# Attention, mixer and MLP on one core: weight chunks, mixer transposes and the first output projection put into later slots

## The chip, the core and the metric

The kernel runs on one core of a Trainium2 chip. Its engines work side by side, each on its own queue of instructions: TensorE (PE, matrix products into PSUM), VectorE (DVE), ScalarE (ACT), GpSimd (POOL) and SyncE (SP). POOL and SP here mostly issue DMAs; the DMAs of both run on the same 16 DMA engines. The metric is the device time of one execution in microseconds, the median of several runs. The kernel before: 818.71 us (three runs, 818.16 to 819.41).

## The reference

A normalised input feeds an attention branch and a mixer-and-MLP branch; the output is the input plus the product of the two.

```python
x = A_x                                     # 2048 tokens x 576
xn = layernorm(x)
# attention: 32 query heads, 16 key/value heads, Dh = 128, the last W = 512 keys of the cache
q = (xn @ wq) by heads
p = softmax(q @ k^T * Dh**-0.5)
s = (p @ v, heads side by side) @ wo        # 4096 -> 576
# mixer and MLP
h  = gelu(layernorm(xn) @ w1)
hs = (four quarters of h shifted by +1, -1, +2, -2 tokens) @ w2
x1 = xn + hs
g  = silu(x1 + gelu(layernorm(x1) @ w3) @ w4)
out = x + s * g
```

## The kernel before

**Blocks and slots.** The 2048 tokens are cut into four blocks (NB = 4) of 512 (QB), each of four tiles (TB) of 128. The attention part is a loop over slots u = 0 to 128, one for each head of each block: Hq = 32 heads, so block b has slots 32 b to 32 b + 31. Slot u has the scores and exponentials of head u (`stage_s`, L545 and L549), the query projection of head u + 1 (`stage_q`, L526, with its rest of 64 rows for four heads at a time in `rest_q`, L511), and the product with the values of head u - 1 (`stage_v`, L564, normalised by DVE at L568 and L569 into an `o` tile).

**What is hung into the slots.** `at(u, fn)` puts work into slot u, `pe(u, atoms)` puts PE work there. The order on SP, POOL and PE is the program's (L723); DVE and ACT are ordered by the framework's scheduler in this part. The lists that the change touches:
- `load_wq(j)` (L335) loads the query weights of four heads, 512 KB and two pieces of 32 KB, into one of two buffers, by POOL in slot 4 (j - 1) - 1. It can go as soon as the last reading of that buffer is over, one slot earlier.
- `load_wo(i)` (L410) loads an eighth of the output projection's weights, 576 KB, by POOL, in slots 9, 13, 17, ... 37 (L673). It goes through `late` (L242): a tiny POOL copy first waits for the first exponential of that slot, and POOL's later DMAs wait behind it.
- `load_k` and `load_v` bring keys and values. The last two groups of four key heads are loaded in slots 4 and 12 into a `stage` buffer, and transposed by DMA from SP in slots 9 to 12 and 17 to 20 (`tr_k`, L380).
- `stage_t(u)` (L574) transposes the `o` tile of a head by DMA from SP into one of 36 `oT` buffers, for the output projection. How many of them are issued in a slot is counted out in L709 to L722: one, two from slot 38 on, and never more than 36 before the first projection is over. There are 18 `o` buffers.
- `wo_groups` (L264): the output projection of a block, four groups of 32 matmuls 512 wide and one of 128 that are 64 wide, each in one slot. The first block's are in slots WO0 = Hq + 11 = 43 to 47, the next ones' in 65 to 69 and 97 to 101. Within a slot the matmuls are dealt out in three parts; the first group already needs all 32 heads and all eight weight chunks.
- `ln2_apply` (L206, two DVE instructions for each tile) normalises a block for the mixer into `xm_b`, and `tr2` (L257) transposes it by DMA from SP. For blocks 0 and 1, `tr2_at` is 34 and 42: the normalisation is written two slots earlier, and the result stays in a `stage` buffer until the mixer. Blocks 2 and 3 have buffers of their own, filled after the loop.
- `load_x` in slots 14, 44 and 68 (`x_at`) loads the next block's input, by POOL through `late`.

**The mixer** comes after the slots (L889 to L953), in an order written by hand on all engines. A loop over k works through sixteen pairs of PSUM banks: `b1_pair` is a product with w1 and its GELU, `b2_pair` a product with w2. Step k issues the first half of pair k, then what `aside` holds for this k, then the second half of pair k - 1 and its evictions. `b1_rest(b)` in `aside` makes the last 64 columns of block b: small products on PE, two DVE instructions (L845, L846), a GELU on ACT (L847) and a transpose by DMA from SP (L848). The banks come round every three steps, so pair 5 starts when the GELUs of pair 2 have read theirs. In step 3, `b1_rest(3)` and the shift copies of block 0 (L855) stand ahead of the second half of pair 2.

After the mixer the MLP runs in matmuls of 64 rows (L1022, L1059), and the last block in 128 (L1237).

Of the kernel before, what the change touches and what calls it, by code (L numbers as in the profile page):

```python
# [8 lines left out]
P = 128  # L9
ACT = mybir.ActivationFunctionType  # L10
ALU = mybir.AluOpType
AX = mybir.AxisListType
BF16 = mybir.dt.bfloat16
# [18 lines left out]
def kernel(  # L32
# [14 lines left out]
    nc = tc.nc  # L47
# [6 lines left out]
    Hq = A_wq.shape[1] // Dh  # L54
# [7 lines left out]
    QB = 512  # L62
    NB = S // QB
    TB = QB // P
# [3 lines left out]
    NDC = NF + 1  # L68
    DP = NDC * P
    DCH = [(i * P, min(P, D - i * P)) for i in range(NDC)]  # L70
    M0 = 512
    R0 = D - M0
# [4 lines left out]
    OFF = 16  # L77
# [150 lines left out]
    oT_pool = octx.enter_context(tc.tile_pool(name="oT_pool", bufs=OT, side="right"))  # L228
    fence_pool = ctx.enter_context(tc.tile_pool(name="fence", bufs=2))
    tctx = ctx.enter_context(ExitStack())  # L230
    stage_pool = tctx.enter_context(tc.tile_pool(name="stage_pool", bufs=2))
    so_pool = tctx.enter_context(tc.tile_pool(name="so_pool", bufs=1))
    so_t, oT_t, xnnT = {}, {}, {}
    w1_all = xT_b[0][:].rearrange("p k q -> p (k q)")
# [16 lines left out]
                                in_=w1_tail.rearrange("p (j two s) -> p j two s", two=2, s=c4)[:, :, half, 0:P])  # L251
    flag_m = [None]

    def stage():
        return stage_pool.tile([P, DP * TB], BF16, name="stage")

    def tr2(b, tt, home=None):  # L257
        if tt == 0:
            xnnT[b] = (home or stage())[:].rearrange("p (k t) -> p k t", k=NDC)
        nc.sync.dma_start(out=xnnT[b][:, :, tt * P:(tt + 1) * P], in_=xm_b[b % 2][:, tt, :], transpose=True)  # L260

    FLAG_OPS = (ALU.max, ALU.min)
# [36 lines left out]
    with ExitStack() as actx:  # L299
# [50 lines left out]
        kst_t = {}  # L350

        def load_k(i, eng=None, step=4):
            kst_t[i] = stage()
            dst = kst_t[i][:, 0:4 * W].rearrange("p (g a) -> p g a", g=4)
            for g in range(0, 4, step):
                (eng or nc.gpsimd).dma_start(
                    out=dst[:, g:g + step, :],
                    in_=A_k_cache[0, 4 * i + g:4 * i + g + step, K0:, :].rearrange("g (p kc) d -> p g (kc d)", p=P))
# [30 lines left out]
        for tt in range(TB):  # L389
            if tt:  # L390
                (nc.sync if tt < TB - 1 else nc.scalar).dma_start(out=x_first[:, tt, :],
                                                                  in_=x2[tt * P:(tt + 1) * P, :])
# [4 lines left out]
        with tc.manual_schedule(engines={SP}):  # L397
            load_k(0, nc.sync, 2)
            for m0 in (0, 2 * Dh):
                cols = slice(m0, m0 + 2 * Dh)  # L400
                nc.sync.dma_start(out=wq_b[0][:, 0:NF, cols],
                                  in_=A_wq[0:NF * P, cols].rearrange("(kc p) m -> p kc m", p=P))
# [220 lines left out]
            return PLAIN - 1 <= u < U - 1 and u % 4 == 3  # L623

        ln2_at = (7, Hq + 3, 2 * Hq - 4, 2 * Hq + 20)
        tr2_at = (Hq + 2, Hq + 10, 3 * Hq - 10, 3 * Hq - 5)
        WO0 = Hq + 11
        tr_k_at = {u: g for u, g in zip([*range(9, 13), *range(17, 21)], range(KDMA, Hkv))}
        x_at = (14, Hq + 12, 2 * Hq + 4)
        ln1_at = (19, Hq + 21, 2 * Hq + 16)  # L630

        for b in range(1, NB):
# [37 lines left out]
                pe_late.append((2 * g - 3, g))  # L670
        for j in range(2, NB * 8):
            at(4 * (j - 1) - 1, lambda j=j: load_wq(j))
        for i, u in enumerate((9, 13, 17, 21, 25, 29, 33, 37)):  # L673
            at(u, lambda i=i, u=u: late(pT_t[u][0][0:1, 0:1], lambda: load_wo(i)))
        for b in range(NB):
            at((b + 1) * Hq + 1, lambda b=b: row_range(b))
# [33 lines left out]
        for u in range(1, U + 1):  # L710
            n = 1
            if u in tr_k_at:
                turn[u] = [lambda g=tr_k_at[u]: tr_k(g)]
                n = 0
            elif u > Hq + 5:
                n = 2
            if u < WO0 + TB + 1:
                n = min(n, OT - done)
            for _ in range(min(n, u - done)):
                turn.setdefault(u, []).append(lambda v=done: stage_t(v))  # L720
                done += 1
# [28 lines left out]
    with ExitStack() as bctx:  # L750
# [23 lines left out]
        hq = mres.tile([P, HW], BF16, name="hq")  # L774
        hs = mres.tile([P, S], BF16, name="hs")
        h4 = [mres.tile([P, TB, P], BF16, name=f"h4_{i}") for i in range(NB)]
# [61 lines left out]
        def b1_rest(b):  # L838
            def ops(half, tt, k):
                w = w1_m[half, k, :].rearrange("p (g s) -> p g s", g=4)[:, :, P:c4] if k < NF else w1_q[half, :, :]  # L840
                return xnnT[b][half, k, tt * P:(tt + 1) * P], w

            pr = small_products(ops)
            gs = gs_pool.tile([P, TB, R0], FP32, name="gs")
            nc.vector.tensor_copy(out=gs[:], in_=pr[0])  # L845
            nc.vector.tensor_tensor(out=gs[:], in0=gs[:], in1=pr[1], op=ALU.add)  # L846
            nc.scalar.activation(out=h4[b][:, :, 0:R0], in_=gs[:], func=ACT.Gelu_apprx_tanh)  # L847
            nc.sync.dma_start(out=hq[:, OFF + b * QB:OFF + (b + 1) * QB].rearrange("p (t q) -> p t q", t=TB),  # L848
                              in_=h4[b][:].rearrange("p t c -> p (t c)"), transpose=True)

        def shifts(b):
            for g in (1, 0, 3, 2):
# [36 lines left out]
        with tc.manual_schedule(engines={SP, POOL, PE, DVE, ACTE}):  # L889
            for b in range(2, NB):  # L890
                home = mres.tile([P, DP * TB], BF16, name=f"xnnT{b}")
                for tt in range(TB):
                    tr2(b, tt, home)
            e = small.tile([P, 1], FP32, name="nr_e")
            nc.scalar.activation(out=e[:], in_=so_t[NB - 1][:, 1, 0:1], func=ACT.Gelu_apprx_tanh)
            for half in range(2):
                nc.gpsimd.dma_start(out=w1_q[HALVES[half], :, :],
                                    in_=w1_tail.rearrange("p (g s) -> p g s", g=4)[:, :, P:c4])
            for half in range(2):
                for g in range(4):  # L900
                    p0 = half * DR + g * rsz
                    nc.gpsimd.dma_start(out=w2_q[p0:p0 + rsz, :], in_=w2_by_g[g, P:c4, :])
            for t in (hb[:, :, OFF - PAD:OFF], hb[:, :, OFF + S:OFF + S + PAD], hq[:, OFF - PAD:OFF],
                      hq[:, OFF + S:OFF + S + PAD], *[t[:, :, R0:] for t in h4]):
                nc.gpsimd.memset(t, 0.0)
            nc.gpsimd.dma_start(out=mx_dram[:, :], in_=flag_m[0][:])
            nc.gpsimd.dma_start(out=m1[:], in_=mx_dram[:, :].rearrange("(o p) c -> o c p", o=1))
            ops = [(b1_pair, 0), (b1_pair, 1), (b2_pair, 0), (b1_pair, 2), (b2_pair, 1), (b1_pair, 3), (b2_pair, 2),
                   (b2_pair, 3)]
            ops = [(f, b, p) for f, b in ops for p in range(2)]  # L910
            aside = {0: [lambda: b1_rest(0)], 1: [lambda: b1_rest(1)], 2: [lambda: b1_rest(2)],
                     3: [lambda: b1_rest(3), lambda: shifts(0)], 6: [lambda: shifts(1)], 8: [lambda: shifts(2)],
                     10: [lambda: shifts(3)]}
            pend = None
            ln3_0 = ln3_steps(0)
            ln3_at = {7: 2, 8: 1, 11: 3, 12: 3}
            for k in range(len(ops) + 1):
                nxt = None
                if k < len(ops):
                    f, b, p = ops[k]  # L920
                    nxt = f(b, p, bank_pair((("pm0", "pm2"), ("pm1", "pm3"))[k % 3 - 1]) if k % 3 else h3_banks())
                    nxt[0]()
                for fn in aside.get(k, []):
                    fn()
                if pend:
                    pend[1]()
                    f, b, p = ops[k - 1]
                    if f is b2_pair and p == 1:
                        b2_rest(b)
                for _ in range(ln3_at.get(k, 0)):  # L930
                    ln3_0.pop(0)()
                pend = nxt
            while ln3_0:
                ln3_0.pop(0)()
            ln3_transpose(0)
            mm = small.tile([1, 2], FP32, name="mm", bufs=1)
            for k in range(2):
                nc.vector.tensor_reduce(out=mm[:, k:k + 1], in_=m1[:, k, :], axis=AX.X, op=FLAG_OPS[k])
            over = small.tile([1, 1], FP32, name="over", bufs=1)
            nc.vector.tensor_scalar(out=over[:], in0=mm[:, 0:1], scalar1=ROW_LIMIT, scalar2=None, op0=ALU.is_gt)  # L940
            nc.vector.scalar_tensor_tensor(out=flag_i[:], in0=mm[:, 1:2], scalar=1.0 / ROW_LIMIT, in1=over[:],
                                           op0=ALU.is_lt, op1=ALU.add)

            def wo_bank(shape, name):
                if name == "pswr":
                    return ps_h2.tile([P, QB], FP32, name="pr0")[:, 0:TB * R0].rearrange("p (t r) -> p t r", t=TB)
                return ps_h2.tile(shape, FP32, name="pr1" if wo_i else "pm0")

            wo_b = wo_groups(NB - 1, wo_bank, nc.scalar)
            for wo_i, i in enumerate((2, TB, 3)):  # L950
                for atom in wo_b[i]:
                    atom()
            nc.gpsimd.tensor_copy(out=gate[:, :], in_=hs[P // 2:P // 2 + 1, S - 1:S])  # L953
# [194 lines left out]
        with tc.manual_schedule(engines={PE, DVE, ACTE}):  # L1148
# [7 lines left out]
            for d in range(0, ND, 2):  # L1156
                b = d // NP
# [3 lines left out]
                end = d % NP == NP - 2  # L1161
# [52 lines left out]
            b = NB - 1  # L1214
# [59 lines left out]
    with tc.If(flag > 0):  # L1274
        nc.gpsimd.dma_start(out=g_dram[(NT - 1) * P:NT * P, :], in_=g_last)
        with ExitStack() as gctx:
# [20 lines left out]
            with tc.For_i(0, NT, 1) as t:  # L1297
# [10 lines left out]
                with tc.For_i(0, Hq, 1) as h:  # L1308
# [7 lines left out]
                                        in_=A_wq[0:NF * P, cols].rearrange("(kc p) m -> p kc m", p=P))  # L1316
# [72 lines left out]
```

## Time and profile before

| | |
|---|---|
| Median of three runs | 818.71 us (818.16 to 819.41) |
| Profiled execution, whole | 822.13 us |
| its span, first to last instruction | 820.6 us |
| Mean granted PE clock | 0.996 |
| PE busy | 806.4 us, 98% |
| DVE, ACT, POOL busy | 445.1, 445.7, 125.2 us |
| DMA queue of SP and ACT (q1), share of 16 engines | 27.4% |
| DMA queue of POOL (q0) | 18.6% |

How the views read: a view of stretches of time has one row for each stretch: its limits and length in us, then the busy time of PE, PE's weight loads (PEld), DVE, ACT and POOL with their number of instructions, the clock granted to PE as a share of full speed, the busy share of the DMA engines, and GB/s. A row of the timeline has the start in us, the duration in us, engine, line, operation, output and inputs, and how many like instructions are merged; in brackets stand the idle time before it and what ended it. A row of DMA issues has the output and input, the engine that issued it, the number, KB for each, and the median time from issue to landing in us. A row of waits has the sum, the number and the longest. A row by line has the shortest, median and longest duration in ns and the first and last start.

### The profile page before, as it was taken

What the parts mean: (1) busy time and instruction counts of PE and PEld (TensorE: products, weight loads), DVE (VectorE), ACT (ScalarE), POOL (GpSimd) and SP (SyncE); (2) the same over time, 40 slices, a digit from 0 to 9 for tenths busy, and PEclk for the clock granted to TensorE, in tenths of its full rate; (3) what the DMA queues carried; (4) which work ended last, traced back from release to release, by engine and by line L of the source; (5) the groups of instructions that cost most, each with busy time, mean ns of one, the idle gap of its engine ahead of it and who ended that gap; (6) DMA issues with size and microseconds to landing.
All of it is one profiled execution on the core that took longest, in us unless ns stands there. A gap on an engine that the chain in (4) does not pass through costs nothing. (4 is left out here: it accounts for less than half of the span.)

```text
span 820.6 us, 19925 instructions
## 1 busy us (share of the span) xinstructions
PE 806.4 (98%) x8174; PEld 466.8 (57%) x8255; DVE 445.1 (54%) x1383; ACT 445.7 (54%) x798; POOL 125.2 (15%) x211
## 2 busy tenths in 40 slices
PE   8998999999999999999999999999999999999997
PEld 6664665566654656645666645655555555555555
DVE  6877686128831579722566528444246636655413
ACT  7887886248833788833788632033233423334620
POOL 3253221101101111100211211172000000000000
PEclk9999999999999999999999999999999999999999
DMA  8899996029821447520553472399000410320101
GB/s 212 143 204 195 171 190 137 29 66 143 156 67 42 91 105 135 110 49 14 107 130 101 79 99 63 66 324 282 3 2 16 77 59 16 48 88 16 45 15 38
DMA packets 135534, 80.73 MB, mean 98 GB/s; under 512 B 112112, under 2 KB 125712, under 8 KB 135440
## 3 DMA queue, kind: packets, MB, share of 16 engines
q1 hardware_dynamic: 121360, 39.32, 27.4%
q0 software_dynamic: 12832, 38.85, 18.6%
q8 instruction: 65, 1.06, 0.6%
q10 hardware_dynamic: 1248, 1.25, 0.5%
q14 instruction: 29, 0.24, 0.1%
HBM read 46.89 MB, written 6.93 MB: 66 GB/s over the span
## 5 line engine op out<-in xcount | busy, mean ns | idle before, releaser
L549 ACT ACTIVATE pT<-sc 128x512 bf16<-128x512 f32 x512 | 287.1, 599 | 96.4 <-PE sc L545 81.6
L545 PE MATMUL sc<-qT,kT 128*128 128x512 bf16 x504 | 167.6, 379 | 0.2
L564 PEld LDWEIGHTS <-pT 128*128 128x128 bf16 x2048 | 134.6, 98 | 53.2 <-issue 11.4
L564 PE MATMUL po<-v_sb,pT 128*128 128x129 bf16 x2048 | 158.3, 220 | 0.5
L526 PE MATMUL psq<-xT_b,wq_b 128*128 128x512 bf16 x455 | 123.2, 381 | 5.3 <-DMA wq_b<-in_A_wq_dram 2.5
L1022 PE MATMUL ph<-xT_b,w_s 64*128 64x512 bf16 x976 | 127.2, 376 | 0.0
L1059 PE MATMUL pm<-w_s,h 64*128 64x512 bf16 x864 | 122.0, 377 | 0.0
L1040 ACT ACTIVATE h<-ph 128x512 bf16<-128x512 f32 x67 | 39.4, 597 | 132.7 <-PE ph L1022 130.5
L569 DVE TENSOR_TENSOR o<-po,ri_b 128x256 bf16<-128x256 f32 x256 | 107.8, 421 | 6.3
L1059 PEld LDWEIGHTS <-h 64*128 64x128 bf16 x1728 | 70.2, 94 | 55.9
L269 PE MATMUL pswo<-wo_sb,oT 128*128 128x512 bf16 x434 | 101.2, 379 | 0.6
L269 PEld LDWEIGHTS <-oT 128*128 128x128 bf16 x1024 | 64.7, 98 | 54.2
L1059 PE MATMUL pr<-w_s,h 64*128 64x64 bf16 x864 | 89.6, 189 | 0.0
L536 DVE CAST qT<-psq 128x512 bf16<-128x512 f32 x64 | 44.0, 688 | 78.1 <-PE psq L511 45.4
L526 PEld LDWEIGHTS <-wq_b 128*128 128x128 bf16 x506 | 49.5, 98 | 61.2 <-DMA wq_b<-in_A_wq_dram 3.0
L1022 PEld LDWEIGHTS <-w_s 64*128 64x128 bf16 x1152 | 55.4, 94 | 49.0 <-issue 0.6
L534 DVE TENSOR_TENSOR qT<-psq,rq 128x512 bf16<-128x512 f32 x62 | 42.8, 690 | 65.1 <-ACT pT L549 57.9
L1038 DVE COPY hx<-ph 128x512 f32<-128x512 f32 x55 | 38.0, 692 | 60.7 <-PE ph L1022 60.7
L339 POOL DMA_DIRECT2D wq_b<-in_A_wq_dram x30 | 23.1, 770 | 272.1 <-PE sc L545 260.3
L568 DVE RECIPROCAL ri_b<-po 128x2 f32<-128x2 f32 x256 | 42.2, 165 | 37.8 <-PE po L564 32.9
L545 PEld LDWEIGHTS <-kT 128*128 128x128 bf16 x512 | 46.0, 98 | 21.1 <-DVE qT L534 0.4
L516 ACT ACTIVATE rq<-sc 128x512 f32<-128x512 f32 x62 | 33.6, 594 | 11.9 <-PE sc L511 11.9
(171 smaller groups left out, 702.1 us busy)
## 6 DMA issues: line engine op xcount, KB each, us to landing
wq_b<-in_A_wq_dram POOLq DMA_DIRECT2D x30, 512.0 KB, 5.2
wo_sb<-in_A_wo_dram POOLq DMA_DIRECT2D x8, 576.0 KB, 5.9
w_s<-in_B_w_dram POOLq DMA_DIRECT2D x9, 512.0 KB, 6.1
w_s<-in_B_w_dram POOLq DMA_DIRECT2D x10, 288.0 KB, 5.1
w_s<-in_B_w_dram POOLq DMA_DIRECT2D x4, 576.0 KB, 5.8
s_b<-s_dram SPq DMA_DIRECT2D x4, 576.0 KB, 5.4
x_b<-in_A_x_dram SPq DMA_DIRECT2D x4, 576.0 KB, 6.7
out_dram<-o SPq DMA_DIRECT2D x15, 144.0 KB, 1.8
```

What stands on the lines that cost most here:

```text
L269: nc.tensor.matmul(ps, lhsT=oT_t[qb * Hq + h][:, tt, :], rhs=wo_sb[:, h, lo:hi], start=(i == 0), stop=(i == Hq - 1))
L526: nc.tensor.matmul(psq[:, :], lhsT=w[:, kc, hh * Dh:(hh + 1) * Dh], rhs=xT_b[qb % 2][:, kc, :], start=(kc == 0 and not (two and hh == 1)), ...
L534: behind["qT"] = nc.vector.tensor_tensor(out=qT[:, :], in0=psq[:, :], in1=rq_t.pop(u)[:, :], op=ALU.add)
L536: nc.vector.tensor_copy(out=qT[:, :], in_=psq[:, :])
L545: nc.tensor.matmul(sc[:, :], lhsT=kT[:, g, kc * P:(kc + 1) * P], rhs=qT_t[u][:, :], start=True, stop=True)
L549: behind["exp"] = nc.scalar.activation(out=pT[:, :], in_=sc[:, :], func=ACT.Exp, scale=SCALE)
L564: nc.tensor.matmul(po[:, j, :], lhsT=pTs[kc][:, tt * P:(tt + 1) * P], rhs=v_sb[:, g, kc, 0:Dh + 1], start=(kc == 0), stop=(kc == KCH - 1))
L568: nc.vector.reciprocal(out=ri, in_=po[:, :, Dh])
L569: nc.vector.tensor_tensor(out=o[:, t0:t0 + 2, :], in0=po[:, :, 0:Dh], in1=ri.unsqueeze(2).to_broadcast([P, 2, Dh]), op=ALU.mult)
L1022: nc.tensor.matmul(ps[i][:, :], lhsT=lhsT, rhs=xT[half, kc, :], start=first, stop=last, skip_group_check=True)
L1040: nc.scalar.activation(out=h3[:, :], in_=src[:, :], func=ACT.Gelu_apprx_tanh)
L1059: nc.tensor.matmul(out, lhsT=h3_t[b, fc][half, tt * P:(tt + 1) * P], rhs=w4_s[fc // WS][half, fc % WS, lo:hi], start=key not in started, s ...
```

## The change

The output projection's weight chunks go from slots 9, 13, 17, 21, 25, 29, 33, 37 to 13, 21, 25, 29, 33, 36, 38, 41. The mixer's normalisations and transposes of blocks 0 and 1 go from slots 32 to 45 to slots 65 to 74. The first output projection starts at slot 45 instead of 43 (WO0), the load of block 2's input goes from slot 44 to 46, and the attention transposes go to two a slot after the first projection, from slot 50, instead of from slot 38. The two rotating `stage` buffers become two buffers with names, chosen by the parity of the group or block. In the mixer, `b1_rest` returns its GELU and transpose as a function `end`; for blocks 0 to 2 it is called at once, for block 3 after the evictions of pair 2.

```diff
@@ -228,7 +228,7 @@
     oT_pool = octx.enter_context(tc.tile_pool(name="oT_pool", bufs=OT, side="right"))
     fence_pool = ctx.enter_context(tc.tile_pool(name="fence", bufs=2))
     tctx = ctx.enter_context(ExitStack())
-    stage_pool = tctx.enter_context(tc.tile_pool(name="stage_pool", bufs=2))
+    stage_pool = tctx.enter_context(tc.tile_pool(name="stage_pool", bufs=1))
     so_pool = tctx.enter_context(tc.tile_pool(name="so_pool", bufs=1))
     so_t, oT_t, xnnT = {}, {}, {}
     w1_all = xT_b[0][:].rearrange("p k q -> p (k q)")
@@ -251,12 +251,12 @@
                                 in_=w1_tail.rearrange("p (j two s) -> p j two s", two=2, s=c4)[:, :, half, 0:P])
     flag_m = [None]
 
-    def stage():
-        return stage_pool.tile([P, DP * TB], BF16, name="stage")
+    def stage(i):
+        return stage_pool.tile([P, DP * TB], BF16, name=f"stage{i % 2}")
 
     def tr2(b, tt, home=None):
         if tt == 0:
-            xnnT[b] = (home or stage())[:].rearrange("p (k t) -> p k t", k=NDC)
+            xnnT[b] = (home or stage(b))[:].rearrange("p (k t) -> p k t", k=NDC)
         nc.sync.dma_start(out=xnnT[b][:, :, tt * P:(tt + 1) * P], in_=xm_b[b % 2][:, tt, :], transpose=True)
 
     FLAG_OPS = (ALU.max, ALU.min)
@@ -350,7 +350,7 @@
         kst_t = {}
 
         def load_k(i, eng=None, step=4):
-            kst_t[i] = stage()
+            kst_t[i] = stage(i)
             dst = kst_t[i][:, 0:4 * W].rearrange("p (g a) -> p g a", g=4)
             for g in range(0, 4, step):
                 (eng or nc.gpsimd).dma_start(
@@ -623,10 +623,10 @@
             return PLAIN - 1 <= u < U - 1 and u % 4 == 3
 
         ln2_at = (7, Hq + 3, 2 * Hq - 4, 2 * Hq + 20)
-        tr2_at = (Hq + 2, Hq + 10, 3 * Hq - 10, 3 * Hq - 5)
-        WO0 = Hq + 11
+        tr2_at = (2 * Hq + 3, 2 * Hq + 7, 3 * Hq - 10, 3 * Hq - 5)
+        WO0 = Hq + 13
         tr_k_at = {u: g for u, g in zip([*range(9, 13), *range(17, 21)], range(KDMA, Hkv))}
-        x_at = (14, Hq + 12, 2 * Hq + 4)
+        x_at = (14, Hq + 14, 2 * Hq + 4)
         ln1_at = (19, Hq + 21, 2 * Hq + 16)
 
         for b in range(1, NB):
@@ -670,7 +670,7 @@
                 pe_late.append((2 * g - 3, g))
         for j in range(2, NB * 8):
             at(4 * (j - 1) - 1, lambda j=j: load_wq(j))
-        for i, u in enumerate((9, 13, 17, 21, 25, 29, 33, 37)):
+        for i, u in enumerate((13, 21, 25, 29, 33, 36, 38, 41)):
             at(u, lambda i=i, u=u: late(pT_t[u][0][0:1, 0:1], lambda: load_wo(i)))
         for b in range(NB):
             at((b + 1) * Hq + 1, lambda b=b: row_range(b))
@@ -712,7 +712,7 @@
             if u in tr_k_at:
                 turn[u] = [lambda g=tr_k_at[u]: tr_k(g)]
                 n = 0
-            elif u > Hq + 5:
+            elif u > WO0 + TB:
                 n = 2
             if u < WO0 + TB + 1:
                 n = min(n, OT - done)
@@ -844,9 +844,15 @@
             gs = gs_pool.tile([P, TB, R0], FP32, name="gs")
             nc.vector.tensor_copy(out=gs[:], in_=pr[0])
             nc.vector.tensor_tensor(out=gs[:], in0=gs[:], in1=pr[1], op=ALU.add)
-            nc.scalar.activation(out=h4[b][:, :, 0:R0], in_=gs[:], func=ACT.Gelu_apprx_tanh)
-            nc.sync.dma_start(out=hq[:, OFF + b * QB:OFF + (b + 1) * QB].rearrange("p (t q) -> p t q", t=TB),
-                              in_=h4[b][:].rearrange("p t c -> p (t c)"), transpose=True)
+
+            def end():
+                nc.scalar.activation(out=h4[b][:, :, 0:R0], in_=gs[:], func=ACT.Gelu_apprx_tanh)
+                nc.sync.dma_start(out=hq[:, OFF + b * QB:OFF + (b + 1) * QB].rearrange("p (t q) -> p t q", t=TB),
+                                  in_=h4[b][:].rearrange("p t c -> p (t c)"), transpose=True)
+
+            if b < NB - 1:
+                end()
+            return end
 
         def shifts(b):
             for g in (1, 0, 3, 2):
@@ -920,10 +926,11 @@
                     f, b, p = ops[k]
                     nxt = f(b, p, bank_pair((("pm0", "pm2"), ("pm1", "pm3"))[k % 3 - 1]) if k % 3 else h3_banks())
                     nxt[0]()
-                for fn in aside.get(k, []):
-                    fn()
+                ends = [fn() for fn in aside.get(k, [])]
                 if pend:
                     pend[1]()
+                    if k == 3:
+                        ends[0]()
                     f, b, p = ops[k - 1]
                     if f is b2_pair and p == 1:
                         b2_rest(b)
```

## The prediction

> **What bounds the kernel now.** I read the page's line of busy times first, then busy time by stretches, then what TensorE (PE) waited for.
>
> ```profile
> PE 806.4 (98%) x8174; PEld 466.8 (57%) x8255; DVE 445.1 (54%) x1383; ACT 445.7 (54%) x798; POOL 125.2 (15%) x211
> 0.00:13.00 13.00, 10.65 (x107) 8.29 (x109) 8.13 (x23) 8.15 (x16) 4.02 (x12) 1.00 0.89 221
> 13.00:75.00 62.00, 61.48 (x555) 38.19 (x564) 48.53 (x164) 54.26 (x99) 25.51 (x41) 1.00 0.95 183
> 75.00:81.00 6.00, 3.31 (x13) 0.83 (x12) 2.67 (x12) 1.75 (x5) 1.21 (x2) 0.72 1.11 190
> 81.00:469.00 388.00, 384.70 (x3333) 227.28 (x3392) 216.97 (x689) 267.23 (x485) 60.01 (x97) 1.00 0.53 102
> 469.00:816.00 347.00, 346.19 (x4175) 192.26 (x4181) 167.99 (x494) 114.10 (x195) 34.49 (x60) 1.00 0.30 74
> 816.00:821.00 5.00, 0.07 (x2) 0.00 (x0) 0.80 (x5) 0.25 (x1) 0.00 (x0) 0.72 0.13 36
> ...
> PE psq L526 <- DMA wq_b<-in_A_wq_dram: 2.5, 1, 2.5
> ...
> PE pm L786 <- ACT hb L812: 0.3, 1, 0.3
> ```
>
> A stretch's row gives its length, then PE, weight loads, DVE, ACT and POOL busy, the granted clock and the DMA share. PE is the bound nearly throughout: over 99% busy except at the start, in the last 5 us, and in the six microseconds from 75 to 81. There it was busy 3.31 of 6.00 us at a mean clock of 0.72. So an edit can only gain where PE stood still, and two such places lie near the change: one wait of 2.5 us for the query-weight DMA, and one of 0.3 us for an ACT eviction.
>
> The stall is longer than its wait, because the clock fell during it:
>
> ```profile
> 75.00:76.00 1.00, 0.49 (x3) 0.00 (x0) 0.93 (x8) 0.93 (x3) 0.00 (x0) 1.00 0.91 305
> 77.00:78.00 1.00, 0.05 (x1) 0.05 (x2) 0.15 (x1) 0.00 (x0) 0.60 (x1) 0.78 0.46 160
> 78.00:79.00 1.00, 0.78 (x2) 0.38 (x4) 0.00 (x0) 0.00 (x0) 0.60 (x1) 0.50 3.85 192
> 79.00:80.00 1.00, 1.00 (x4) 0.13 (x4) 0.00 (x0) 0.00 (x0) 0.00 (x0) 0.50 0.19 68
> 80.00:81.00 1.00, 1.00 (x7) 0.26 (x4) 0.59 (x1) 0.16 (x1) 0.00 (x0) 0.52 0.17 66
> ```
>
> From 78 to 81 PE ran at half clock and lost 0.50 + 0.50 + 0.48 = 1.48 us. With the wait of 2.5 that is 4.0. The query-weight loads confirm it independently. They are issued once per four heads, so their spacing is four slots:
>
> ```profile
> 57.65 1.53 POOL L362 DMA_DIRECT2D v_sb<-in_A_v_cache_dram  x2 [1.67 <-DMA wo_sb<-in_A_wo_dram]
> ...
> 60.28 0.75 POOL L412 DMA_DIRECT2D wo_sb<-in_A_wo_dram  x1 [0.31 <-issue]
> 62.56 0.75 POOL L339 DMA_DIRECT2D wq_b<-in_A_wq_dram  x1 [1.53 <-PE sc L545]
> ...
> 73.80 0.75 POOL L339 DMA_DIRECT2D wq_b<-in_A_wq_dram  x1 [1.59 <-PE sc L545]
> ...
> 88.99 0.75 POOL L339 DMA_DIRECT2D wq_b<-in_A_wq_dram  x1 [1.50 <-PE sc L545]
> ...
> 100.18 0.76 POOL L339 DMA_DIRECT2D wq_b<-in_A_wq_dram  x1 [0.53 <-PE sc L545]
> ```
>
> 100.18 - 88.99 = 11.19 us is the undisturbed spacing; 88.99 - 73.80 = 15.19. The difference, 4.00 us, is what the stall cost. A slot is 2.8 us here.
>
> **Why that load was late.** The load issued at 62.56 (written in slot 19, free one slot earlier) holds heads 24 to 27; PE wants it in slot 23, about 75.3. What was queued around it, with the time from issue to landing:
>
> ```profile
> v_sb<-in_A_v_cache_dram POOLq DMA_DIRECT2D x1, 128.0 KB, 14.7
> ...
> wo_sb<-in_A_wo_dram POOLq DMA_DIRECT2D x1, 576.0 KB, 16.4
> ...
> wq_b<-in_A_wq_dram POOLq DMA_DIRECT2D x1, 512.0 KB, 15.3
> ```
>
> The value load was the second of the two at 57.65, issued near 58.4: it landed at 58.4 + 14.7 = 73.1. The output-projection chunk of slot 17 landed at 60.28 + 16.4 = 76.7, and the query weights at 62.56 + 15.3 = 77.9. They land in order of issue on one queue, in a time when the DMA share is 0.95 or more.
>
> **The change, part by part.**
>
> *Weight chunks.* Before: slots 9, 13, 17, 21, 25...; after: 13, 21, 25, 29, 33, 36, 38, 41. Up to the critical load only the chunk of slot 13 remains ahead. The chunk that goes is the one issued at 60.28, directly ahead of it. How much earlier the query weights land isn't in the trace, so I bound it. The upper bound is what the chunk took at the head of the queue: 76.7 - 73.1 = 3.6 us, giving a landing at 74.3, before 75.3. The lower bound is what a load of like size took right behind it: 77.9 - 76.7 = 1.2 us, giving 76.7, still 1.4 late. I take 3.6, the row of the chunk itself in its own place, while the 1.2 belongs to a moment when the queue ran free again. Speaking for it, too, is the other chunk that goes, slot 9's:
>
> ```profile
> 37.17 0.75 POOL L412 DMA_DIRECT2D wo_sb<-in_A_wo_dram  x1
> ...
> 47.92 0.78 POOL L356 DMA_DIRECT2D stage<-in_A_k_cache_dram  x1 [6.00 <-DMA kT<-stage]
> ```
>
> POOL stood 6.0 us at the last key load for key transposes that shared the engines with that chunk. Some of this should come back; I count nothing for it.
>
> [...]
>
> So this term is -4.0 us, wait and half clock together. What is late next: the four chunks written in slots 33 to 41 lie closer than before, with query loads in slots 35, 39 and 43 between them. Each query load has about 12.7 us (62.56 to 75.3) until it is wanted. In the tightest later place of the old schedule it took
>
> ```profile
> wq_b<-in_A_wq_dram POOLq DMA_DIRECT2D x1, 512.0 KB, 9.8
> ```
>
> (issued at 111.34, while eight mixer transposes shared the engines, which now leave this stretch). Margin 2.9 us: cost 0, and a repeat of the old stall, 4.0, if the cover is gone. The last chunk, slot 41, is wanted in the last third of slot 45, over four slots or 11 us on; even 9.8 would do.
>
> *Mixer transposes of blocks 0 and 1.* Moved, not removed: eight DMA transposes on SP and the normalisations before them on DVE.
>
> ```profile
> L260 SPq DMA_TRANSPOSE stage<-xm_b x8: 1199/1254/2169, 101.8 to 129.4; - x8
> ...
> L209 DVE TENSOR_SCALAR xm_b<-xn_b,ln_mv,ln_r x32: 279/354/430, 42.5 to 331.8; 128x576 bf16<-128x576 bf16 x16, 128x64 bf16<-128x64 bf16 x16
> ...
> 237.00:257.00 20.00, 19.89 (x117) 9.75 (x117) 3.67 (x10) 6.73 (x12) 1.97 (x3) 1.00 0.16 43
> ```
>
> 8 x 1.25 = 10 us of SP issue and 16 x 0.354 = 5.7 us of DVE. Slots 65 to 69 are the second output projection, where (last row) DVE is busy 3.67 of 20 us and DMA 16%: hidden, cost 0. Without that cover DVE would hold an attention slot by up to 4 x 0.354 = 1.4 us, four instructions being one slot's share. The result is first read near 481 us, so lateness costs nothing.
>
> *First output projection at slot 45, input load at 46, attention transposes doubled only from slot 50.* PE does the same matmuls in another order: 0. What changes is the backlog on SP. Before, slot 47 left 11 untransposed heads; after, slot 49 leaves 13, and 18 output buffers hold them. Before:
>
> ```profile
> 181.85 29.45 SPq L577 DMA_TRANSPOSE oT<-o  x20
> 211.40 5.29 SPq L461 DMA_TRANSPOSE xT_b<-xn_b  x4
> 216.78 8.77 SPq L577 DMA_TRANSPOSE oT<-o  x6
> ```
>
> The projection ends two slots, about 5.2 us, later in program time, and 16 transposes instead of 20 stand ahead of the four of the next block (4 x 1.3 = 5.2 less), so those go out at the same moment; four heads are pushed behind them. Head 63 then leaves SP as the twelfth from 216.78: 216.78 + 11 x 1.31 = 231.2. Normal landing there:
>
> ```profile
> oT<-o SPq DMA_TRANSPOSE x9, 2.9
> ...
> 235.16 2.54 PE L269 MATMUL pswo<-wo_sb,oT 128*128 128x512 bf16 x11
> ```
>
> It is wanted by the last of these eleven matmuls, about 237.3; it lands at 234.1. Cost 0, margin 3.2 us.
>
> *Two named key buffers.* The allocations alternated between two buffers already; the same tile follows the same tile. 0.
>
> *The fourth block's small activation after the pair.*
>
> ```profile
> 487.95 1.07 ACT L812 ACTIVATE hb<-pm 128x512 bf16<-128x512 f32 x2
> 490.45 0.42 ACT L847 ACTIVATE h<-gs 128x256 bf16<-128x256 f32 x1 [1.43 <-DVE gs L846]
> 490.77 1.06 ACT L812 ACTIVATE hb<-pm 128x512 bf16<-128x512 f32 x2
> ...
> 490.57 1.03 PE L786 MATMUL ph<-stage,xT_b 64*128 64x512 bf16 x8
> 491.88 1.90 PE L786 MATMUL pm<-xT_b,hb 64*128 64x512 bf16 x16 [0.28 <-ACT hb L812]
> ```
>
> ACT idles 1.43 us for a DVE sum before the pair that PE needs. Eight such matmuls take 0.87 us from start to start, so PE should go on at 491.44 and did at 491.88: 0.44 lost. With the pair first, it starts near 489.9 and ends by 491.0. Gain 0.44. The transpose behind the small activation goes out some 0.5 us later and is read much later: 0. The bounds are 0 (if DVE's fence behind the shift copies is the next wait) and 0.44.
>
> **The sum.** On the profiled execution: 822.13 - 4.00 - 0.44 = 817.7. That execution lies 3.42 us above the median of the plain runs, 818.71, though PE streams alike; the excess must lie where PE doesn't stream: the first 13 us, the stall's 4.0 and the last 5. Shared by length, 3.42 x 4.0 / 22 = 0.6 us of the stall would exist only under the profiler. Gain in plain runs 3.4 + 0.44 = 3.8, hence 814.9.
>
> **Rivals.**
>
> *A. The stall only shrinks.* By the 1.2 us: wait 1.4 left, half clock kept, gain 1.2 + 0.44 = 1.64: 817.1. For: landings 1.2 apart. Against: 3.6 for the chunk itself. [...]
>
> *B. Plain runs hardly have the stall.* If all 3.42 us of the excess sit in it, 0.6 are left to win, plus 0.44: 817.7, no measurable change. For: the excess itself, and that the stall is a DMA race. Against: the start and the tail wait on DMA too.
>
> *C. Slower: SP's longer backlog.* Place: last third of slot 65, head 63. It decides once that transpose takes over 237.3 - 231.2 = 6.1 us to land; transposes beside a full queue took
>
> ```profile
> oT<-o SPq DMA_TRANSPOSE x1, 17.5
> ```
>
> (issued at 59.03). Halfway, at 13, PE would wait 6.9 and lose 1.5 to the clock: 814.9 + 8.4 = 823.3. Against: 2.9 in that place, DMA share 16% after it.
>
> **How the numbers follow.** Forecast 0.58, A 0.12, B 0.22, C 0.08. 0.2% is 1.6 us, about what a measurement of this kernel tells from no change, so the edge is 817.1: the forecast and half of A are faster (0.64), the rest of A and B the same (0.28), C slower. Range 813.7 to 818.3: below, the full 4.44 and half a microsecond of scatter; above, B and as much scatter. C is left out.
>
> **What would show it.** Right: no PE wait for query weights between 60 and 90 us, clock 1.00 there, query loads 11.2 apart throughout, the load after slot 18 landing within 12.7 us; ACT's pair ahead of the small activation and PE going on without the 0.44. A: a shorter wait at the same place. C: PE idle near slot 65's end, released by a transpose. Wrong altogether: new DMA waits in slots 35 to 47, or a span 4 us shorter with the plain median unmoved (B).

## The result and the profile after

The changed kernel took 824.05 us (median of 22 executions, 820.49 to 831.87); the kernel before, on the same chips, 819.18 (22 executions, 817.67 to 826.92). The ratio is 1.0058, 95% interval 1.0039 to 1.0077: slower by 0.6%, where 814.9 and faster was forecast, and outside the range. The profiled execution took 829.59 us with a span of 828.0, before 822.13 and 820.6.

Of the profile after, first what PE waited for, then the stretches around the two large waits (columns as before: length, PE, weight loads, DVE, ACT, POOL busy, granted clock, DMA share, GB/s):

```profile
PE po L564 <- DVE o L569: 4.5, 1, 4.5
PE psq L526 <- DMA wq_b<-in_A_wq_dram: 3.9, 1, 3.9
```

```profile
13.00:63.00 50.00, 50.00 (x457) 30.81 (x456) 37.99 (x123) 43.68 (x80) 18.61 (x29) 1.00 0.99 159
63.00:72.00 9.00, 5.11 (x33) 2.32 (x32) 3.00 (x10) 3.37 (x8) 3.48 (x5) 0.81 1.08 212
72.00:281.00 209.00, 209.00 (x1824) 121.35 (x1822) 114.48 (x382) 135.20 (x246) 36.85 (x63) 1.00 0.57 111
281.00:291.00 10.00, 5.48 (x32) 2.87 (x31) 3.42 (x12) 3.15 (x6) 0.00 (x0) 0.83 0.55 123
291.00:824.00 533.00, 532.56 (x5816) 305.06 (x5813) 277.86 (x833) 252.16 (x446) 62.35 (x102) 1.00 0.36 81
```

Between 13 and 824 us PE streams nearly without a gap outside two stretches. In the first it stood 9.00 - 5.11 = 3.9 us for query weights and lost 9 x 0.19 = 1.7 us to the clock: the old stall, one load earlier (the load written in slot 15, wanted in slot 19; before, the one of slot 19, wanted in 23). In the second it stood 4.5 us for DVE and lost 10 x 0.17 = 1.7: a new one. The wait of 0.3 us for ACT in the mixer is gone from the list.

What DVE did in the second, from its timeline:

```profile
279.10 0.69 DVE L536 CAST qT<-psq 128x512 bf16<-128x512 f32 x1 [1.20 <-PE psq L511]
285.31 0.64 DVE L209 TENSOR_SCALAR xm_b<-xn_b,ln_mv,ln_r 128x576 bf16<-128x576 bf16 x2 [5.52 <-DMA stage<-xm_b]
285.86 0.16 DVE L568 RECIPROCAL ri_b<-po 128x2 f32<-128x2 f32 x1
286.06 0.42 DVE L569 TENSOR_TENSOR o<-po,ri_b 128x256 bf16<-128x256 f32 x1
```

DVE stood 5.52 us at a normalisation (L209) until a mixer transpose had landed, and did the evictions that PE wanted (L568, L569) right behind it. Those evictions had had their input, the `po` of L564, since about 280.5 us. The normalisation is block 2's, written for slots 84 and 85. Blocks 0 and 2 share `xm_b0`: it writes the buffer that block 0's transposes still have to read. Those transposes are the moved ones. SP's timeline and two landings show why the last of the four was so late:

```profile
275.41 0.38 SPq L284 DMA_DIRECT2D s_dram<-so  x1
275.89 2.85 SPq L577 DMA_TRANSPOSE oT<-o  x1
278.80 1.26 SPq L260 DMA_TRANSPOSE stage<-xm_b  x1
```

```profile
s_dram<-so SPq DMA_DIRECT2D x1, 576.0 KB, 5.4
...
stage<-xm_b SPq DMA_TRANSPOSE x1, 6.5
```

It stood on SP behind the store of the second projection and an attention transpose, went out at 278.80 and landed 6.5 us later, at 285.3. SP itself had stood at that store until ACT had done the projection's last eviction; of its waits between 262 and 283 us:

```profile
SPq L284 <- ACT so L291: 8.6, 1, 8.6
```

So the last transpose could only go out when the projection, PE's other work in these slots, was over.

### The profile page after: what moved, and what is told of

It reads as the page before. It is cut to its first block, busy times and chain, and to the rows that moved or that the text cites. A ratio compares the mean times of both kernels' runs of the same rounds, so it can differ in the third digit from the quotient of the medians.

```text
span 828.0 us, 19994 instructions
## 1 busy us (share of the span) xinstructions
PE 813.2 (98%) x8255; PEld 471.1 (57%) x8255; DVE 445.6 (54%) x1383; ACT 445.8 (54%) x798; POOL 125.3 (15%) x211
## 5 line engine op out<-in xcount | busy, mean ns | idle before, releaser
L545 PE MATMUL sc<-qT,kT 128*128 128x512 bf16 x512 | 171.6, 381 | 0.0
L564 PEld LDWEIGHTS <-pT 128*128 128x128 bf16 x2048 | 135.3, 98 | 58.3 <-issue 12.0
L564 PE MATMUL po<-v_sb,pT 128*128 128x129 bf16 x2048 | 159.3, 221 | 4.6 <-DVE o L569 4.5
L526 PE MATMUL psq<-xT_b,wq_b 128*128 128x512 bf16 x506 | 130.8, 381 | 3.9 <-DMA wq_b<-in_A_wq_dram 3.9
L569 DVE TENSOR_TENSOR o<-po,ri_b 128x256 bf16<-128x256 f32 x256 | 107.7, 421 | 6.4
L269 PE MATMUL pswo<-wo_sb,oT 128*128 128x512 bf16 x448 | 103.2, 379 | 0.0
L568 DVE RECIPROCAL ri_b<-po 128x2 f32<-128x2 f32 x256 | 42.1, 164 | 39.1 <-PE po L564 34.3
```

The costliest lines, as they stand in the source:

```text
L269: nc.tensor.matmul(ps, lhsT=oT_t[qb * Hq + h][:, tt, :], rhs=wo_sb[:, h, lo:hi], start=(i == 0), stop=(i == Hq - 1))
L526: nc.tensor.matmul(psq[:, :], lhsT=w[:, kc, hh * Dh:(hh + 1) * Dh], rhs=xT_b[qb % 2][:, kc, :], start=(kc == 0 and not (two and hh == 1)), ...
L545: nc.tensor.matmul(sc[:, :], lhsT=kT[:, g, kc * P:(kc + 1) * P], rhs=qT_t[u][:, :], start=True, stop=True)
L564: nc.tensor.matmul(po[:, j, :], lhsT=pTs[kc][:, tt * P:(tt + 1) * P], rhs=v_sb[:, g, kc, 0:Dh + 1], start=(kc == 0), stop=(kc == KCH - 1))
L568: nc.vector.reciprocal(out=ri, in_=po[:, :, Dh])
L569: nc.vector.tensor_tensor(out=o[:, t0:t0 + 2, :], in0=po[:, :, 0:Dh], in1=ri.unsqueeze(2).to_broadcast([P, 2, Dh]), op=ALU.mult)
```

## The experiments

**Two ways to free DVE.** The first puts the mixer work of blocks 0 and 1 back; the second leaves it late and only orders block 2's normalisation on DVE.

```diff
 a_tr2_old (on the changed kernel)
-        tr2_at = (2 * Hq + 3, 2 * Hq + 7, 3 * Hq - 10, 3 * Hq - 5)
+        tr2_at = (Hq + 2, Hq + 10, 3 * Hq - 10, 3 * Hq - 5)
 b_hold (on the changed kernel)
+        def held(b, tt):
+            with tc.issue_after(behind["qT"].ins) if b == 2 else ExitStack():
+                ln2_apply(b, tt)
 ...
-                at(tr2_at[b] - 2 + tt // 2, lambda b=b, tt=tt: ln2_apply(b, tt))
+                at(tr2_at[b] - 2 + tt // 2, lambda b=b, tt=tt: held(b, tt))
```

In `held`, `behind["qT"]` is the latest eviction of a query projection: block 2's normalisation is put behind it on DVE.

> The changed kernel with the mixer's normalisations and transposes of blocks 0 and 1 back in slots 32 to 45; all else as changed. Theory 1 (DVE reaches block 2's normalisation early, which overwrites the buffer that block 0's late transposes still read, and its queue stands): the PE wait on DVE o (4.5 us near 282) and the half clock behind it are gone, span 828.0 - 6.4 = 821.6 if the query-weight stall stays as in the changed kernel, plain time about 6 us under the changed kernel's 824, so 818. Rival (two extra transposes in the backlog of SP, or the later output projection, make DVE late): the wait near 282 stays, 824 or more.

> The changed kernel, mixer transposes late as changed, but block 2's normalisation is ordered on DVE behind a query eviction of its own slots 84 and 85. Theory 1: no DVE wait near 282, span about 821.6, plain about 818, like the run with the old slots. Rival (the late transposes themselves, by crowding SP and the DMA engines, make PE wait): a wait of some us between 270 and 300 stays, plain 822 or more.

Measured: 817.65 us (10 executions, 817.25 to 822.62; ratio to before 0.9983, interval 0.9959 to 1.0007) and 817.92 (10, 817.41 to 818.91; 0.9983, 0.9965 to 1.0002). Both profiled spans are 815.9. In the kernel with the order held the only wait of PE left is at the start:

```profile
PE warm L687 <- POOL ident masks.py:199: 1.9, 1, 1.9
```

So it is the order on DVE together with the shared buffer; the late transposes on SP and the DMA engines cost PE no wait by themselves. Neither profiled execution had the query-weight stall either, which I had not expected (two of the ten timed ones with the old slots lie higher, at 820.4 and 822.62): 828.0 - 815.9 = 12.1 us is both stalls, 3.9 + 1.7 + 4.5 + 1.7 = 11.8 by the rows above.

**The late transposes alone.**

```diff
 d_tr2_late (on the kernel before)
-        tr2_at = (Hq + 2, Hq + 10, 3 * Hq - 10, 3 * Hq - 5)
+        tr2_at = (2 * Hq + 3, 2 * Hq + 7, 3 * Hq - 10, 3 * Hq - 5)
```

> The kernel before with the mixer's normalisations and transposes of blocks 0 and 1 alone put into slots 65 to 74. Theory 1: a PE wait on DVE of 4 to 5 us around slot 69 to 71 and 3.4 us of half clock behind it, 6 us slower than before in plain runs (825). Rival (it takes the later output projection as well): no such wait, 819.

Measured: 826.26 us (10 executions, 821.08 to 830.28), ratio 1.0062, interval 1.0033 to 1.0091. The wait is there without any other part of the change:

```profile
PE po L564 <- DVE o L569: 4.3, 1, 4.3
PE psq L526 <- DMA wq_b<-in_A_wq_dram: 3.2, 1, 3.2
```

```profile
282.58 0.64 DVE L209 TENSOR_SCALAR xm_b<-xn_b,ln_mv,ln_r 128x576 bf16<-128x576 bf16 x2 [5.27 <-DMA stage<-xm_b]
```

**The same wait in a place with cover.** Two slots earlier, block 0's last transpose stands in slot 68, ahead of the store.

```diff
 e_tr2_65 (on the changed kernel)
-        tr2_at = (2 * Hq + 3, 2 * Hq + 7, 3 * Hq - 10, 3 * Hq - 5)
+        tr2_at = (2 * Hq + 1, 2 * Hq + 5, 3 * Hq - 10, 3 * Hq - 5)
```

> The changed kernel with the mixer's transposes of blocks 0 and 1 two slots earlier (65 to 72): block 0's last one then stands in slot 68, inside the long slots of the second output projection and ahead of the store of its result. Theory 1 (DVE stands behind the buffer, and that costs only where PE has attention work alone): DVE still waits for the transposes, but in the projection's slots, PE has no wait near 282, span about 816 if the query weights come in time, plain about 817.7. Rival (late transposes cost wherever they are, by SP or DMA): some us of PE wait between 228 and 300, plain 821 or more.

Measured: 817.92 us (10 executions, 817.66 to 825.81), ratio 0.9989, interval 0.9959 to 1.002; span 816.3. DVE still stands, four times:

```profile
231.10 0.64 DVE L209 TENSOR_SCALAR xm_b<-xn_b,ln_mv,ln_r 128x576 bf16<-128x576 bf16 x2 [4.14 <-DMA stage<-xm_b]
236.24 0.64 DVE L209 TENSOR_SCALAR xm_b<-xn_b,ln_mv,ln_r 128x576 bf16<-128x576 bf16 x2 [3.97 <-DMA stage<-xm_b]
242.70 0.64 DVE L209 TENSOR_SCALAR xm_b<-xn_b,ln_mv,ln_r 128x576 bf16<-128x576 bf16 x2 [3.95 <-DMA stage<-xm_b]
252.88 0.64 DVE L209 TENSOR_SCALAR xm_b<-xn_b,ln_mv,ln_r 128x576 bf16<-128x576 bf16 x2 [3.95 <-DMA stage<-xm_b]
```

Some 4 us each, and PE has no wait for DVE: it has projection matmuls to do. The changed kernel shows the same within one trace: DVE's first three waits there, 3.96 to 3.97 us each and the last over at 268.1, fell into projection slots and cost PE nothing; only the fourth did. That fourth wait is longer as well: its transpose went out beside the store and took 6.5 us to landing, where the median of the eight is 2.7, so place and length changed together here. In the three traces that have it, PE's wait is DVE's less 1.0 us (5.52 and 4.5; 5.27 and 4.3; 4.61 and 3.6, the last in the second trace of the changed kernel, below), so 4 us in an attention slot would cost about 3, an estimate that no run tests.

**Is the query-weight stall part of the change?** The changed kernel again, unedited:

> The changed kernel once more, for a second trace. If the query-weight stall at 64 us belongs to the change, it is there again (PE wait of 3 to 5 us). If it is a race that this execution lost, as the runs without any PE wait suggest, it is gone or elsewhere, and the DVE wait near 282 remains: span 822 to 823.

Measured: 823.9 us, span 822.4, and of the two stalls only DVE's:

```profile
PE po L564 <- DVE o L569: 3.6, 1, 3.6
```

```profile
wq_b<-in_A_wq_dram POOLq DMA_DIRECT2D x1, 512.0 KB, 4.2
```

The second fence is the query load of slot 19: 4.2 us to landing, 15.3 before. The one of slot 15 took 8.0 here and 14.2 in the profile above. So the stall at 64 us is a race that this program loses in some executions: the same load of the same program lands before PE wants it in one, and after it in another. The kernel before, too, spreads widely. In four comparisons it ran 95 times: 47 lie between 817.6 and 819.5 us, the other 48 between 819.5 and 826.9. The profiled 822.13 lies in the upper half. That the query weights make the spread of the executions without a trace is inferred from the next runs.

**Which weight chunk makes the query weights late.**

```diff
 g_wo17 and h_wo9 (on the kernel before)
-        for i, u in enumerate((9, 13, 17, 21, 25, 29, 33, 37)):
+        for i, u in enumerate((9, 13, 21, 23, 25, 29, 33, 37)):      # g_wo17
+        for i, u in enumerate((13, 17, 21, 25, 29, 31, 33, 37)):     # h_wo9
```

> The kernel before with one weight chunk moved: the one of slot 17 goes to slot 23 (the two behind it stay 21 and then 23, 25: chunks in 9, 13, 21, 23, 25, 29, 33, 37). Theory 2 (the chunk issued right ahead of the query weights of slot 19 made them late): these land within 6 us of issue, hardly any execution above 819.5, stall-free level 818.1 as before. Rival (slot 9's chunk does it, by holding the key transposes and POOL): query weights still land 12 us or more after issue, and as many executions above 819.5 as before (11 of 25).

> The kernel before with slot 9's chunk taken away from the front and the chunks of 13 and 17 left where they are (13, 17, 21, 25, 29, 31, 33, 37). Theory 2: the chunk of slot 17 still stands ahead of the query weights, they land 10 us or more after issue and several of ten executions lie above 819.5. Rival (slot 9's chunk does it): no such execution, landing within 6 us.

Measured without slot 17's chunk: 819.39 us, 10 executions from 817.52 to 820.3. The median is no lower than before's 819.14, and three of ten still lie above 819.5, but the long executions are gone (none above 820.3, ten of 25 before), and the ratio is 0.9966, interval 0.9942 to 0.999. Without slot 9's: 822.38, six of ten between 821.74 and 827.63; ratio 1.0027, 0.9994 to 1.006. The load of slot 19 took 10.5, 15.3 and 15.9 us to landing in three of the four traces with slot 17's chunk ahead of it (PE waited 3.2 us for it in the fourth, the late transposes alone), and 4.1 to 9.0 in the eight without. So slot 17's chunk makes the long stall, as the prediction had it. But the forecast of 6 us was a miss: the load of slot 19 took 9.0, and PE waited a little for the one before it, that of slot 15 (10.5 us to landing):

```profile
PE psq L511 <- DMA wq_b<-in_A_wq_dram: 0.9, 1, 0.9
...
PE psq L526 <- DMA wq_b<-in_A_wq_dram: 0.2, 1, 0.2
```

```profile
wq_b<-in_A_wq_dram POOLq DMA_DIRECT2D x1, 512.0 KB, 10.5
```

With both chunks moved, these landings were 8.3 (slot 15) and 4.2 us (slot 19) in the kernel with the order held. The other kernel's own profiled execution, with slot 17's chunk in place, happened to be one without the stall (10.5 us, no wait).

**The deferred activation alone.**

```diff
 c_defer (on the kernel before: the last two parts of the diff, nothing else)
```

> The kernel before with the fourth block's small activation alone put behind the pair's evictions. Theory: ACT's pair runs before the small activation, PE starts the next product without the 0.44 us gap, the span shrinks by 0.4 apart from what the query-weight stall does. Rival: DVE's fence behind the shift copies is the next wait and PE stands as long.

Measured: 822.54 us once, span 821.0, with a query-weight wait of 3.0 us that hides a gain of half a microsecond. The place itself is clear:

```profile
490.73 1.08 ACT L812 ACTIVATE hb<-pm 128x512 bf16<-128x512 f32 x2 [0.89 <-PE pm L786]
491.71 0.42 ACT L848 ACTIVATE h<-gs 128x256 bf16<-128x256 f32 x1
```

```profile
491.40 1.03 PE L786 MATMUL ph<-stage,xT_b 64*128 64x512 bf16 x8
492.26 2.10 PE L786 MATMUL pm<-xT_b,hb 64*128 64x512 bf16 x16
```

ACT runs the pair first, and PE goes on 0.86 us after the eight matmuls began, where it took 1.31 before: 0.45 us. The lowest times lie as far apart, 817.64 in 95 executions before and 817.19 with the deferral, but that proves little: without slot 17's chunk, and without the deferral, the lowest was 817.52.

**A version faster than the kernel before.** The order held, timed longer; and with block 1's input moved behind the query weights of slot 15.

```diff
 k_hold5: b_hold again
 i_x16 (on b_hold)
-        x_at = (14, Hq + 14, 2 * Hq + 4)
+        x_at = (16, Hq + 14, 2 * Hq + 4)
```

> The changed kernel with block 2's normalisation held to its slots, timed longer against the kernel before. Theory: no DVE wait, the query weights of slot 19 within 6 us of issue, 817.8 plain; the kernel before loses in about half of its executions, so the ratio is 0.998 with an interval below 1. Rival (the ten executions were lucky): two or three in ten above 820, ratio 1.000.

> The same, with block 1's input loaded in slot 16 instead of 14, so that the query weights of slot 15 are issued ahead of it on POOL. Theory 3 (what is left of the race is the input standing ahead of these weights): they land by 60 us, no execution above 819.5, 817.6. Rival: now the input lands too late for DVE's statistics of slot 19 to 21, DVE stands, and PE waits for it near 66 us: 819 or more.

Measured: 817.66 us (12 executions, 817.19 to 822.66, two above 820), ratio 0.9968, interval 0.9943 to 0.9993; and 817.55 (10, 817.19 to 818.09), 0.9959, 0.9939 to 0.998. The median before was 820.76 in this comparison, the highest of the four, which helps both ratios. The first's profiled execution lost the race by a little, a landing at 53.7 + 12.1 = 65.8:

```profile
PE psq L526 <- DMA wq_b<-in_A_wq_dram: 1.8, 1, 1.8
```

In the second, four input loads no longer stand ahead:

```profile
wq_b<-in_A_wq_dram POOLq DMA_DIRECT2D x1, 512.0 KB, 7.5
```

Issued at 51.27 it lands at 58.8, five microseconds before PE wants it, and the input (4.0 us to landing) is still in time. All ten executions lie within 0.9 us. With both chunks moved, and DVE free or covered, seven of 42 executions in four runs lay above 819.5, here none of ten. That the input was the rest of the race fits the landing; ten executions don't prove it.

## Why the prediction was wrong, step by step

*The step that failed* is in the mixer transposes: "The result is first read near 481 us, so lateness costs nothing", and "hidden, cost 0". It asked who reads the result, and not who next writes the source. `xm_b0` is written again for block 2, and the kernel before had shown that this happens early: its normalisations of block 2, written in slots 84 and 85 (about 313 us, estimated from the third projection's start in slot 97 near 350 us and 2.8 us a slot), ran in slots 64 and 65.

```profile
226.32 0.97 DVE L209 TENSOR_SCALAR xm_b<-xn_b,ln_mv,ln_r 128x576 bf16<-128x576 bf16 x3
```

Even the row quoted in the prediction said so: its first start, 42.5 us, belongs to an instruction written for slot 32. DVE has no handwritten order in this loop, and the scheduler puts these instructions in long before their slots. The change did not even move the normalisations of blocks 0 and 1, of which the prediction put 5.7 us of DVE into slots 65 to 69. Block 0's first stands where it stood, at 42.42 us after and 42.50 before, and block 1's begin at 126.25 and 124.76; only the transposes moved. The row of the same line after:

```profile
L209 DVE TENSOR_SCALAR xm_b<-xn_b,ln_mv,ln_r x32: 278/384/430, 42.4 to 339.6; 128x576 bf16<-128x576 bf16 x16, 128x64 bf16<-128x64 bf16 x16
```

The term of 0 measured 4.5 + 1.7 = 6.2 us in the trace. At the medians it is 824.05 - 817.66 = 6.4 us between the changed kernel and the same with DVE's order held, which ran in different comparisons, and 826.26 - 818.87 = 7.4 in the run that had it alone, where the race of the query weights adds its scatter to both sides. The fallback price in that step, 1.4 us for four instructions, was for the wrong thing: the instructions' duration, not the wait of the one at the head of the queue.

*The weight chunks, -4.0.* The mechanism was right: slot 17's chunk makes the load of slot 19 late, and with it gone the load lands in 4 to 9 us and not in 15. The size was wrong, in two ways. The stall is a race. Medians of the kernel before were 818.9 to 820.8 in the four comparisons, the kernels without stalls 817.6, and 0.45 of that is the deferral: the chunks are worth 818.9 - 817.6 - 0.45 = 0.8 to 820.8 - 817.6 - 0.45 = 2.7 us at the median, about 1.1 or less in three of the four, nearer to rival B's 0.6 than to 3.4. Sharing the profiled execution's excess of 3.42 us by length was the step: without the stall of 4.0 that execution would have taken 822.13 - 4.0 = 818.1, so the excess was nearly all stall. And the load of slot 15, whose landing at 53.9 + 9.9 = 63.8 left hardly any margin before, wasn't weighed; it is the one that came late in the profile after.

*The deferral, -0.44:* right, 0.45 measured. *First projection two slots later, fewer doubled transposes, named buffers:* right at 0; with DVE's order held PE shows no wait for them, so rival C's place (slot 65) saw nothing. Rival C had the sign and the neighbourhood, a few slots off, and the wrong engine: not an SP backlog that PE waits for, but an SP backlog that DVE waits for. That its 823.3 comes near the measured 824.05 is luck: it is 8.4 us added to a base of 814.9 that wasn't reached.

*The chances.* 0.08 for slower was too little for a kernel in which PE has no slack and a transfer is moved past the next writer of its source.

## What to carry to other kernels

When a transfer is put later, look for the next writer of its source as well as the readers of its result, and find where that writer really stands on its engine: in a scheduled stream by its start in the trace, not by its place in the program. Here DVE, waiting for a buffer, held everything behind it: four such waits of 3.95 to 4.14 us cost PE nothing where it had projection matmuls to do, and one of 5.52 us cost it 4.5 where it had attention work alone. And before a stall in one profile is priced, see whether other executions have it: the profiled execution here lay 3.42 us above the median of a kernel that otherwise streams, and it was one that had lost a race.

## What the runs showed of the hardware

*DVE kept its order.* The evictions that PE waited for had their inputs from about 280.5 us, and DVE stood 5.52 us, until 285.3, for the instruction ahead of them.

*Half the clock for 3.4 us, after some stalls.* Two stalls of the same kernel, the late transposes alone, differ:

```profile
75.00:78.00 3.00, 0.14 (x1) 0.00 (x0) 1.90 (x7) 1.31 (x3) 1.36 (x2) 1.00 0.84 258
...
80.00:81.00 1.00, 1.00 (x18) 0.88 (x17) 1.00 (x5) 1.00 (x3) 0.00 (x0) 1.00 0.13 47
...
284.00:285.00 1.00, 1.00 (x18) 0.92 (x16) 0.97 (x4) 0.31 (x1) 0.00 (x0) 0.95 0.00 0
285.00:286.00 1.00, 1.00 (x5) 0.43 (x4) 0.92 (x3) 0.64 (x2) 0.00 (x0) 0.50 0.47 94
...
288.00:289.00 1.00, 1.00 (x14) 0.88 (x13) 0.72 (x3) 0.60 (x1) 0.00 (x0) 0.85 0.65 131
```

3.2 us of waiting left the clock at 1.00; after 4.3 us it was 0.50 for 0.1 + 3 + 0.3 = 3.4 us. Yet in the kernel before a wait of 2.5 us was enough for 0.44 + 2 + 0.96 = 3.4 us, by the rows in the prediction (0.78, 0.50, 0.50, 0.52 from 77 to 81 us). What decides it no run here shows. So the price of a stall of 2.5 to 3.2 us has a step in it that the stall's length doesn't settle: 1.48 us in the kernel before, 3.4 x 0.50 = 1.7 after the 4.3.
